# The head of a fused transformer block: six of sixteen input tiles transposed on TensorE, the LayerNorm scale split over three engines, the large head loads on one queue

## The chip, the cores and the metric

The kernel runs on one core of one Trainium2 chip. The metric is device time in microseconds (us) of one execution. Before the change it was 1218.61 us (median of its first three runs, 1215.19 to 1218.82).

The engines are named as the profile names them: PE is TensorE's matmul, PEld its weight load (the two overlap), DVE is VectorE, ACT is ScalarE, POOL is GpSimd and SP is SyncE. In this kernel SP only starts DMA transfers.

## The reference, cut to what matters

```python
x = A_x                                        # 1 x 2048 x 1024, bf16
h = x + attention(layernorm(x), wq, wk, wv, wo)   # 32 query heads of 32, ONE key/value head
h2 = h + mlp(layernorm(h), w_gate, w_up, w_down)  # sigmoid(g) * u, 3584 hidden columns

def _layernorm(x, axis=-1, eps=1e-5):
    m = jnp.mean(x, axis=axis, keepdims=True)
    v = jnp.var(x, axis=axis, keepdims=True)
    return (x - m) / jnp.sqrt(v + eps)
```

The 2048 rows are 16 tiles of 128 rows. Softmax in the attention covers all 2048 keys, so every tile of x must be normalised, transposed and multiplied by wk and wv before the first PV product can run.

## The kernel before

The program is written by a small planner. It holds a guess of each instruction's duration, walks through the work by priority, and so fixes, once and for all, the order of the instructions on each engine. On the chip each engine runs its own list in that order and waits on semaphores. A time that changes on the chip does not reorder anything, but a change in the planner's input does.

The head (the part that the change touches) loads x on two queues, computes the statistics, normalises in two passes, and transposes each tile by a DMA:

```python
load_x([0], SP, "sp"); load_x([1], SP, "sp"); load_x([2, 3], SP, "sp")
# wk, wv: on ACT's queue
load_x([4, 5, 6, 7], ACT, "act")
load_wq(0)                                 # ACT's queue
load_x([8, 9, 10, 11], ACT, "act")
load_x([12, 13, 14, 15], ACT, "act")
load_wq(1)                                 # ACT's queue
warm = pl.op("act", lambda: ACT.activation(out=tnh[:, 0, 0:1], in_=half, func=ACTF.Exp), ...)
wo_ld = dma(lambda: SP.dma_start(wo_sb[:, :, :], ...), "wo", D * D * 2, [x_ld[12]], prio=4)
...
for ts in [[0], [1]] + [[t, t + 1] for t in range(2, NT, 2)]:
    sv = stats(0, ts, ...)                 # DVE: bn_stats; POOL: two powers give rstd
    for t in ts:
        cen = ... DVE.tensor_scalar(..., scalar1=mvr[:, 0, t, 0:1], op0=ALU.subtract) ...
        if t < 1 or t >= 10:
            xnorm[t] = ... DVE.tensor_scalar(..., scalar1=rstd[:, 0, t:t + 1], op0=ALU.mult) ...
        else:
            xnorm[t] = ... ACT.activation(..., func=ACTF.Copy, scale=rstd[:, 0, t:t + 1]) ...
        xT_ev[t] = dma(lambda t=t: SP.dma_start_transpose(
            out=xnT4[t // 4][:, :, (t % 4) * P:(t % 4 + 1) * P], in_=x_sb[:, t, :]), ...)
```

After that, five kinds of TensorE work run. They are named in the order of the planner's priorities:

```python
PRIO = ["KV", "Q0", "PV", "OP", "D", "GU", "Q"]
```

KV and Q are the projections (KV gives the keys and the values). Then there are the scores and PV, the attention proper, with an exp on ScalarE between them. OP is the output projection of a tile, GU the gate and up half of the MLP, D its down half. The MLP goes in *chunks*: tile 0 and tile 1 alone, then two tiles at a time.

The softmax here doesn't subtract the row's maximum and nothing guards it: scores larger than these inputs give would overflow.

Of the kernel before, what the change touches and what calls it, by code (L numbers as in the profile page):

```python
# [35 lines left out]
class Plan:  # L36
# [39 lines left out]
    def step(self, limit):  # L76
        best = None
        for e in self.ENG:
            h = self.heap[e]
            if h:  # L80
                s = max(self.free[e], min(o.ready for o in h))
                if best is None or s < best[0]:
                    best = (s, e)
        if best is None or (limit is not None and best[0] > limit):
            return False
        s, e = best
        h = self.heap[e]
        o = min((o for o in h if o.ready <= s + 1e-9), key=lambda o: (o.prio, o.seq))
        h.remove(o)
        self.free[e] = s + o.occ  # L90
        if o.nbytes:
            go = max(s + 1300.0, self.dma_free[e])
            self.dma_free[e] = go + o.nbytes / 260.0
            o.end = self.dma_free[e] + 700.0
        else:
            o.end = s + o.lat
        o.pos = len(self.lists[e])
        self.lists[e].append(o)
        for u in o.users:
            u.ready = max(u.ready, o.end)  # L100
            u.missing -= 1
            if u.missing == 0:
                self.heap[u.eng].append(u)
        o.users = []
        return True
# [22 lines left out]
def bass_sequential_preLN__grouped_kv_mqa__glu_gated_glu__prompt_kernel(  # L128
# [34 lines left out]
    with ExitStack() as es:  # L163
# [5 lines left out]

        zone = SB("zone", [NFT * D])  # L170
# [52 lines left out]
        def dma(fn, key, nbytes, deps=(), prio=5, ring="sp"):  # L223
            return pl.op(ring, fn, deps, occ=520.0, key=key, nbytes=nbytes, prio=prio)
# [15 lines left out]
        c_v1 = pl.op("pool", lambda: POOL.memset(Vaug[:, :, DH:DH + 1], 1.0), [c1], occ=100)  # L240
# [4 lines left out]
        def load_x(ts, eng, ring):  # L245
            sl = slice(ts[0] * P, (ts[-1] + 1) * P)
            o = dma(lambda: eng.dma_start(x_sb[:, ts[0]:ts[-1] + 1, :], xf[sl, :].rearrange("(a p) n -> p a n", p=P)),
                    f"x{ts[0]}", P * D * 2 * len(ts), prio=0, ring=ring)
            for t in ts:
                x_ld[t] = o  # L250

        def load_wq(k):
            wq_ld.append(dma(lambda: ACT.dma_start(
                wq_sb[:, :, k * 512:(k + 1) * 512],
                A_wq[:, k * 512:(k + 1) * 512].rearrange("(a p) n -> p a n", p=P)), f"wq{k}", D * 512 * 2, prio=0,
                ring="act"))

        load_x([0], SP, "sp")
        load_x([1], SP, "sp")
        load_x([2, 3], SP, "sp")  # L260
# [4 lines left out]
        load_x([4, 5, 6, 7], ACT, "act")  # L265
        load_wq(0)
        load_x([8, 9, 10, 11], ACT, "act")
        load_x([12, 13, 14, 15], ACT, "act")
        load_wq(1)
        warm = pl.op("act", lambda: ACT.activation(out=tnh[:, 0, 0:1], in_=half, func=ACTF.Exp), [c0], prio=1, occ=1400)  # L270
        wo_ld = dma(lambda: SP.dma_start(wo_sb[:, :, :], A_wo.rearrange("(g p) n -> p g n", p=P)), "wo", D * D * 2,
                    [x_ld[12]], prio=4)
# [45 lines left out]
        xT_ev = {}  # L318
        for ts in [[0], [1]] + [[t, t + 1] for t in range(2, NT, 2)]:
            sv = stats(0, ts, [x_sb[:, t, :] for t in ts], [[x_ld[t]] for t in ts], 3)  # L320
            for t in ts:
                cen = pl.op("dve", lambda t=t: DVE.tensor_scalar(
                    out=x_sb[:, t, :], in0=x_sb[:, t, :], scalar1=mvr[:, 0, t, 0:1], scalar2=None, op0=ALU.subtract),
                    [sv[0]], prio=2, occ=400, lat=560)
                if t < 1 or t >= 10:
                    xnorm[t] = pl.op("dve", lambda t=t: DVE.tensor_scalar(
                        out=x_sb[:, t, :], in0=x_sb[:, t, :], scalar1=rstd[:, 0, t:t + 1], scalar2=None, op0=ALU.mult),
                        [cen, sv[1]], prio=1, occ=400, lat=560)
                else:
                    xnorm[t] = pl.op("act", lambda t=t: ACT.activation(  # L330
                        out=x_sb[:, t, :], in_=x_sb[:, t, :], func=ACTF.Copy, scale=rstd[:, 0, t:t + 1]),
                        [cen, sv[1]], prio=1, **t_act(1024))
                xT_ev[t] = dma(lambda t=t: SP.dma_start_transpose(
                    out=xnT4[t // 4][:, :, (t % 4) * P:(t % 4 + 1) * P], in_=x_sb[:, t, :]), f"xT{t}", P * D * 2, [xnorm[t]], prio=0)
# [8 lines left out]
        PRIO = ["KV", "Q0", "PV", "OP", "D", "GU", "Q"]  # L343

        def mm(o, l, r, start, stop, **kw):
            return lambda: PE.matmul(o, lhsT=l, rhs=r, start=start, stop=stop, **kw)  # L346

# [170 lines left out]
        def mk_PV(G):  # L518
# [12 lines left out]
            def after(b, last):  # L531
# [11 lines left out]
                if g == NG - 1:  # L543
                    ot_ev[qb] = dma(lambda: SP.dma_start_transpose(out=OT[:, qb % 2, :, :], in_=Osb[:, qb % 2, :]),
                                    f"OT{qb % 2}", P * D * 2, [o_ev[qb * NG + i] for i in range(NG)] + [op_last.get(qb - 2)],
                                    prio=0)
# [54 lines left out]
        def flush_hT():  # L601
            while late_hT and (CHUNK_OF[late_hT[0]] == 0 or (CHUNK_OF[late_hT[0]] - 1) in gu_last):
# [4 lines left out]
                    [hnorm[t], gu_last.get(c - 1)], prio=0)  # L607
# [86 lines left out]
        for t in range(NT):  # L694
            queue_after_xT(t)
        for t in range(2):
            load_xr(t, [])
        for s in range(NSLAB):
            load_slab(s, [xT_ev[k] for k in range(4 * s, 4 * s + 4)] if s < 4 else [xT_ev[NT - 1]])
# [168 lines left out]
```

## Time and profile before

| | before |
|---|---|
| time | 1218.61 us |
| PE busy | 1143.3 us of 1219.1 (94%) |
| ACT busy | 1041.3 us (85%) |
| PE idle in the first 80 us | 33.8 us |
| first projection matmul | 24.97 us |

These lines are from the page of the kernel before: the busy table, and the table of 40 slices, each 30.5 us wide, with the busy share in tenths.

```profile
span 1219.1 us, 47282 instructions
PE 1143.3 (94%) x21988; PEld 820.6 (67%) x22080; DVE 289.2 (24%) x788; ACT 1041.3 (85%) x1316; POOL 38.4 (3%) x82
...
PE   1889888989889999999999999999999999999998
...
ACT  2769988999999999999999999999999999991120
...
PEclk9989998999899999999999999999999999999999
DMA  8972499299136551566326651568135650579480
```

PE's first slice is the worst.

The waits of PE in the first 80 us, as total us, times, longest:

```profile
PE F_ps L346 <- DMA zone<-ring: 26.6, 3, 25.0
PE F_ps L346 <- ACT QTb L235: 4.0, 4, 1.6
PE F_ps L346 <- issue: 2.7, 1, 2.7
```

`zone<-ring` is the DMA transpose of a normalised x tile. The first projection takes tiles 0 and 1 together, so it waits for both transposes, until 25.0 us. Two lines of the chain that ended last show where these 25 us went, as start, us, what: the load of x, then the transposes.

```profile
1.84 9.02 DMA ring<-in_A_x_dram
...
14.72 10.01 DMA zone<-ring
```

Tile 1 was normalised, and its transpose issued, at 14.7 us; the result came 10 us later. The windows view gives 46.24 us of PE busy in the first 80:

```profile
sum 80.00, PE 46.24 PEld 32.76 DVE 38.09 ACT 40.88 POOL 16.85; mean PE 5.78 PEld 4.09 DVE 4.76 ACT 5.11 POOL 2.11
```

ScalarE's timeline (start, us, instruction) shows its own late start. It was held by issuing large loads until 10.9 us:

```profile
4.02 4.64 ACTq L247 DMA_DIRECT2D ring<-in_A_x_dram  x2
8.69 2.21 ACTq L253 DMA_DIRECT2D zone<-in_A_wq_dram  x1
10.93 1.28 ACT L270 ACT_TABLE_LOAD   x1 [10.93 <-issue]
```

### The profile page before, as it was taken

Reading aid. Unit: us, or ns where it says so; the run is one execution under the profiler, and the core shown is the slowest. Engines: PE = TensorE matmul, PEld = TensorE weight load, DVE = VectorE, ACT = ScalarE, POOL = GpSimd, SP = SyncE. Lnnn points to the kernel's source line nnn. Section 1 sums busy time; section 2 is a strip of 40 time slices with the busy share of each in tenths; the row PEclk is TensorE's granted clock in tenths of the full one; section 3 lists DMA queues with packets and bytes.
Section 4 is the critical chain, followed back from the end, with each engine's and each line's share of the span. In section 5 each row is a group of like instructions: output and inputs, shape, how many; then the busy total and the mean of one; then the engine's idle time right before and its main releaser. Section 6 shows DMA issues by size and latency. Waiting matters only on the chain.

```text
span 1219.1 us, 47282 instructions
## 1 busy us (share of the span) xinstructions
PE 1143.3 (94%) x21988; PEld 820.6 (67%) x22080; DVE 289.2 (24%) x788; ACT 1041.3 (85%) x1316; POOL 38.4 (3%) x82
## 2 busy tenths in 40 slices
PE   1889888989889999999999999999999999999998
PEld 1645576676568765877577865787567865787684
DVE  8222211222121312121212112221212221222121
ACT  2769988999999999999999999999999999991120
POOL 4100000000000000000000000000000000000000
PEclk9989998999899999999999999999999999999999
DMA  8972499299136551566326651568135650579480
GB/s 263 227 209 95 130 271 266 67 252 250 48 89 180 152 136 41 153 176 168 73 80 158 175 144 33 149 183 186 52 80 158 179 141 15 115 193 219 112 213 18
DMA packets 338308, 178.29 MB, mean 146 GB/s; under 512 B 58304, under 2 KB 328640, under 8 KB 338112
## 3 DMA queue, kind: packets, MB, share of 16 engines
q1 hardware_dynamic: 332368, 169.90, 54.1%
q10 hardware_dynamic: 5744, 5.37, 1.3%
q8 instruction: 173, 2.83, 1.0%
q14 instruction: 23, 0.19, 0.0%
HBM read 155.32 MB, written 7.34 MB: 133 GB/s over the span
## 4 chain that ended last, share of the span: by engine, by line
PE 85%; ACT 7%; issue 3%; DMA 3%; DVE 1%; ACTq 0%; DVEq 0%
PE F_ps L346 72%; PE S_ps L346 13%; ACT Pr L503 6%; DMA zone<-ring 2%; DMA ring<-in_A_x_dram 1%; DMA q_scratch<-hact 1%; ACT tnh L647 1%; ACT ring L330 1%; DVE hact L654 0%; DMA hnT<-hn 0%; DVE st L285 0%; DVE st L287 0%; DVE h_sb L580 0%; ACT QTb L235 0%; DVE mv L289 0%
## 5 line engine op out<-in xcount | busy, mean ns | idle before, releaser
L503 ACT ACTIVATE Pr<-S_ps 128x1024 bf16<-128x1024 f32 x1024 | 977.9, 1042 | 39.6 <-PE S_ps L346 38.7
L346 PE MATMUL F_ps<-hnT,ring 128*128 128x256 bf16 (+1 forms) x4032 | 445.9, 262 | 4.7 <-issue 1.6
L346 PEld LDWEIGHTS F_ps<-hnT,ring 128*128 128x128 bf16 x4032 | 340.6, 98 | 61.3 <-issue 5.9
L346 PE MATMUL F_ps<-Vaug,Pr 128*128 128x33 bf16 x8192 | 244.9, 178 | 9.8 <-issue 7.3
L346 PEld LDWEIGHTS F_ps<-Vaug,Pr 128*128 128x128 bf16 x8192 | 229.6, 96 | 35.9 <-issue 8.9
L346 PE MATMUL S_ps<-QTb,kT 32*128 32x128 bf16 x8192 | 208.8, 218 | 18.5 <-ACT Pr L503 10.9
L346 PEld LDWEIGHTS S_ps<-QTb,kT 32*128 32x128 bf16 x8192 | 119.7, 93 | 130.7 <-ACT Pr L503 73.5
L346 PE MATMUL F_ps<-zone,hact 128*128 128x512 bf16 x843 | 203.2, 380 | 3.8 <-issue 1.8
L654 DVE SCALAR_TENSOR_TENSOR hact<-tnh,F_ps 128x256 bf16<-128x256 f32 (+1 forms) x252 | 97.7, 391 | 445.0 <-ACT tnh L647 436.6
L647 ACT ACTIVATE tnh<-F_ps 128x256 f32<-128x256 f32 (+1 forms) x252 | 94.5, 380 | 81.3 <-PE F_ps L346 81.3
L346 PEld LDWEIGHTS F_ps<-zone,hact 128*128 128x128 bf16 x896 | 78.9, 98 | 88.5 <-DVE hact L654 0.3
L346 PE MATMUL F_ps<-zone 128*128 128x256 bf16 (+2 forms) x497 | 73.2, 294 | 31.9 <-DMA zone<-ring 26.6
L346 PEld LDWEIGHTS F_ps<-zone 128*128 128x128 bf16 x512 | 38.5, 99 | 53.3 <-issue 27.5
L686 DVE SCALAR_TENSOR_TENSOR h_sb<-F_ps,h_sb 128x512 bf16<-128x512 f32 x32 | 22.1, 692 | 199.4 <-PE F_ps L346 199.4
L346 PE MATMUL F_ps<-wo_sb,OT 128*128 128x512 bf16 x232 | 60.7, 390 | 4.1 <-issue 2.1
L536 DVE RECIPROCAL rL<-F_ps 128x4 f32<-128x4 f32 x128 | 23.4, 183 | 149.2 <-PE F_ps L346 149.1
L299 POOL TENSOR_SCALAR zb<-mvb 128x1 bf16<-128x1 bf16 (+1 forms) x25 | 5.6, 224 | 1073.3 <-DVE mvb L295 1073.3
L346 PEld LDWEIGHTS F_ps<-wo_sb,OT 128*128 128x128 bf16 x256 | 22.0, 99 | 25.4 <-issue 4.9
L538 DVE TENSOR_TENSOR Osb<-F_ps,rL 128x128 bf16<-128x128 f32 x128 | 37.3, 291 | 4.3
L580 DVE TENSOR_TENSOR h_sb<-F_ps,xres 128x512 bf16<-128x512 f32 x32 | 22.1, 692 | 56.3 <-PE F_ps L346 56.3
L236 DVE CAST hact<-F_ps 128x512 bf16<-128x512 f32 x24 | 16.6, 692 | 39.4 <-PE F_ps L346 37.3
L306 POOL TENSOR_TENSOR rstd<-dsb,cst 128x1 f32<-128x1 bf16 (+1 forms) x25 | 16.7, 667 | 1.9
(27 smaller groups left out, 116.7 us busy)
## 6 DMA issues: line engine op xcount, KB each, us to landing
ring<-in_B_w_gate_dram SPq DMA_DIRECT2D x126, 512.0 KB, 4.2
ring<-in_B_w_up_dram SPq DMA_DIRECT2D x126, 512.0 KB, 5.8
zone<-in_B_w_down_dram SPq DMA_DIRECT2D x7, 1024.0 KB, 7.6
xres<-in_A_x_dram SPq DMA_DIRECT2D x16, 256.0 KB, 2.7
out_dram<-h_sb SPq DMA_DIRECT2D x32, 128.0 KB, 1.7
ring<-in_A_x_dram ACTq DMA_DIRECT2D x3, 1024.0 KB, 12.6
q_scratch<-hact SPq DMA_DIRECT2D x24, 128.0 KB, 2.4
QTb<-q_scratch SPq DMA_DIRECT2D x6, 512.0 KB, 3.5
```

Of the source, the lines that this page charges most:

```text
L236: lambda: DVE.tensor_copy(out=out_ap, in_=in_ap))
L299: f = pl.op("pool", lambda: POOL.tensor_scalar(out=zb[:, ph, sl].unsqueeze(2), in0=mvb[:, ph, sl, 1:2], scalar1=LN_EPS_BF16, scalar2=None, ...
L306: h = pl.op("pool", lambda: POOL.tensor_tensor(out=rstd[:, ph, sl], in0=dsb[:, ph, sl], in1=nb, op=ALU.pow), [g, c1], prio=prio - 1, occ=5 ...
L330: xnorm[t] = pl.op("act", lambda t=t: ACT.activation(out=x_sb[:, t, :], in_=x_sb[:, t, :], func=ACTF.Copy, scale=rstd[:, 0, t:t + 1]), [ce ...
L346: return lambda: PE.matmul(o, lhsT=l, rhs=r, start=start, stop=stop, **kw)
L503: exps[u] = pl.op("act", lambda slot=slot, pb=pb: ACT.activation(out=Pr[:, slot, :].rearrange("p (a b) -> p a b", a=2), in_=S_ps[:, pb:pb ...
L536: a = pl.op("dve", lambda: DVE.reciprocal(rL[:, k, :].unsqueeze(2), ov[:, :, DH:DH + 1]), [last], prio=0, occ=70, lat=280)
L538: e = pl.op("dve", lambda: DVE.tensor_tensor(out=Osb[:, qb % 2, g * P:(g + 1) * P].rearrange("p (a b) -> p a b", a=4), in0=ov[:, :, 0:DH], ...
L580: h_ev[(t, dc)] = pl.op("dve", lambda: DVE.tensor_tensor(out=h_sb[:, t % 4, sl], in0=F_ps[:, b, :], in1=xres[:, t % 2, sl], op=ALU.add), [ ...
L647: a = pl.op("act", lambda: ACT.activation(out=tnh[:, k, 0:n], in_=F_ps[:, b, 0:n], func=ACTF.Tanh, scale=0.5), [last, tn_user.get(k)], pri ...
L654: e = pl.op("dve", lambda: DVE.scalar_tensor_tensor(out=hactT[:, ft, 0:n], in0=tnh[:, k, 0:n], scalar=1.0, in1=F_ps[:, b, 256:256 + n], op ...
L686: e = pl.op("dve", lambda: DVE.scalar_tensor_tensor(out=h_sb[:, t % 4, sl], in0=F_ps[:, b, :], scalar=0.5, in1=h_sb[:, t % 4, sl], op0=ALU ...
```

## The change

The intent is to let TensorE begin earlier: tiles 0 to 5 are transposed on TensorE, so they do not queue among DMA loads; ScalarE issues only the two small loads; ScalarE and VectorE give some of the scaling to GpSimd; and the weights that are needed later are loaded behind the transposes. The planner's guesses of DMA time are adjusted too (bandwidth 260 to 280, a DMA transpose's issue 520 to 1330 ns), and so is that of a VectorE pass over a tile (400 to 360 ns).

```diff
-            self.dma_free[e] = go + o.nbytes / 260.0
+            self.dma_free[e] = go + o.nbytes / 280.0
...
-        load_x([4, 5, 6, 7], ACT, "act")
+        load_x([2, 3])                    # all load_x and load_wq on SP now
+        load_x([4, 5])
+        load_x([6, 7])
         load_wq(0)
...
-        wo_ld = dma(..., [x_ld[12]], prio=4)
...
+        SCALE_ON = ["dve"] + ["act"] * 3 + ["pool"] * 2 + ["act"] + ["pool"] * 2 + ["act"] + ["pool"] * 2 + ["dve"] * 4
...
+        wo_ld = dma(..., [xnorm[NT - 1]], prio=4)
...
-        PRIO = ["KV", "Q0", "PV", "OP", "D", "GU", "Q"]
+        PRIO = ["xT", "KV", "Q0", "PV", "OP", "D", "GU", "Q"]
...
+        def mk_xT(t):                     # eight 128x128 transposes into one PSUM bank
+            ...
+                return [(lambda dt=dt: PE.transpose(out=tp[:, dt * P:(dt + 1) * P],
+                                                    in_=x_sb[:, t, dt * P:(dt + 1) * P], identity=ident[:, :]),
+                         P, []) for dt in range(DT)]
+            ...
+                xT_ev[t] = pl.op("act", fa, [last], prio=2, **t_act(1024))    # evicted by ScalarE
+                if t == NPT - 1:          # then the ten DMA transposes, then the MLP weight slabs
+                    for k in range(NPT, NT):
+                        dma_xT(k)
+                    for k in range(4):
+                        load_slab(k, ...)
...
+        NPT = 6
```

More of the change, by code (lines that the diff above doesn't have):

```diff
@@ L168, in SB @@
             return EC(nc.sbuf_tensor(name, [P] + shape, dt))
+        ident = SB("ident", [P])
         zone = SB("zone", [NFT * D])
@@ L221, in bass_sequential_preLN__grouped_kv_mqa__glu_gated_glu__prompt_kernel, with dma @@
         PE, ACT, DVE, POOL, SP = nc.tensor, nc.scalar, nc.vector, nc.gpsimd, nc.sync
-        def dma(fn, key, nbytes, deps=(), prio=5, ring="sp"):
-            return pl.op(ring, fn, deps, occ=520.0, key=key, nbytes=nbytes, prio=prio)
+        def dma(fn, key, nbytes, deps=(), prio=5, ring="sp", occ=520.0):
+            return pl.op(ring, fn, deps, occ=occ, key=key, nbytes=nbytes, prio=prio)
         def evac(fn_act, fn_dve, n, deps, prio, dve_rate=0.96):
@@ L239, in bass_sequential_preLN__grouped_kv_mqa__glu_gated_glu__prompt_kernel, with load_x @@
         c1 = pl.op("pool", lambda: POOL.memset(negone, -1.0), [c0], occ=60)
-        c_v1 = pl.op("pool", lambda: POOL.memset(Vaug[:, :, DH:DH + 1], 1.0), [c1], occ=100)
+        c2 = pl.op("pool", lambda: POOL.memset(ident[:, :], 0.0), [c1], occ=200)
+        c_id = pl.op("pool", lambda: POOL.affine_select(
+            out=ident[:, :], in_=ident[:, :], compare_op=ALU.not_equal, fill=1.0, base=0,
+            pattern=[[-1, P]], channel_multiplier=1), [c2], occ=300)
+        c_v1 = pl.op("pool", lambda: POOL.memset(Vaug[:, :, DH:DH + 1], 1.0), [c_id], occ=100)
         x_ld = {}
         wq_ld = []
-        def load_x(ts, eng, ring):
+        def load_x(ts):
             sl = slice(ts[0] * P, (ts[-1] + 1) * P)
-            o = dma(lambda: eng.dma_start(x_sb[:, ts[0]:ts[-1] + 1, :], xf[sl, :].rearrange("(a p) n -> p a n", p=P)),
-                    f"x{ts[0]}", P * D * 2 * len(ts), prio=0, ring=ring)
+            o = dma(lambda: SP.dma_start(x_sb[:, ts[0]:ts[-1] + 1, :], xf[sl, :].rearrange("(a p) n -> p a n", p=P)),
+                    f"x{ts[0]}", P * D * 2 * len(ts), prio=0)
             for t in ts:
@@ L252, in load_wq @@
         def load_wq(k):
-            wq_ld.append(dma(lambda: ACT.dma_start(
+            wq_ld.append(dma(lambda: SP.dma_start(
                 wq_sb[:, :, k * 512:(k + 1) * 512],
-                A_wq[:, k * 512:(k + 1) * 512].rearrange("(a p) n -> p a n", p=P)), f"wq{k}", D * 512 * 2, prio=0,
-                ring="act"))
-        load_x([0], SP, "sp")
-        load_x([1], SP, "sp")
-        load_x([2, 3], SP, "sp")
+                A_wq[:, k * 512:(k + 1) * 512].rearrange("(a p) n -> p a n", p=P)), f"wq{k}", D * 512 * 2, prio=0))
+        load_x([0])
+        load_x([1])
         wk_ld = dma(lambda: ACT.dma_start(wk_sb, A_wk.rearrange("(a p) j -> p a j", p=P)), "wk", P * DT * DH * 6, prio=0,
@@ L264, in bass_sequential_preLN__grouped_kv_mqa__glu_gated_glu__prompt_kernel @@
                     ring="act")
-        load_x([4, 5, 6, 7], ACT, "act")
+        load_x([2, 3])
+        load_x([4, 5])
+        load_x([6, 7])
         load_wq(0)
-        load_x([8, 9, 10, 11], ACT, "act")
-        load_x([12, 13, 14, 15], ACT, "act")
+        load_x([8, 9])
+        load_x([10, 11])
+        load_x([12, 13, 14, 15])
         load_wq(1)
         warm = pl.op("act", lambda: ACT.activation(out=tnh[:, 0, 0:1], in_=half, func=ACTF.Exp), [c0], prio=1, occ=1400)
-        wo_ld = dma(lambda: SP.dma_start(wo_sb[:, :, :], A_wo.rearrange("(g p) n -> p g n", p=P)), "wo", D * D * 2,
-                    [x_ld[12]], prio=4)
         rep = None
@@ L321, in bass_sequential_preLN__grouped_kv_mqa__glu_gated_glu__prompt_kernel @@
             for t in ts:
-                cen = pl.op("dve", lambda t=t: DVE.tensor_scalar(
-                    out=x_sb[:, t, :], in0=x_sb[:, t, :], scalar1=mvr[:, 0, t, 0:1], scalar2=None, op0=ALU.subtract),
-                    [sv[0]], prio=2, occ=400, lat=560)
-                if t < 1 or t >= 10:
-                    xnorm[t] = pl.op("dve", lambda t=t: DVE.tensor_scalar(
-                        out=x_sb[:, t, :], in0=x_sb[:, t, :], scalar1=rstd[:, 0, t:t + 1], scalar2=None, op0=ALU.mult),
-                        [cen, sv[1]], prio=1, occ=400, lat=560)
-                else:
-                    xnorm[t] = pl.op("act", lambda t=t: ACT.activation(
-                        out=x_sb[:, t, :], in_=x_sb[:, t, :], func=ACTF.Copy, scale=rstd[:, 0, t:t + 1]),
-                        [cen, sv[1]], prio=1, **t_act(1024))
-                xT_ev[t] = dma(lambda t=t: SP.dma_start_transpose(
-                    out=xnT4[t // 4][:, :, (t % 4) * P:(t % 4 + 1) * P], in_=x_sb[:, t, :]), f"xT{t}", P * D * 2, [xnorm[t]], prio=0)
+                xt, sc = x_sb[:, t, :], rstd[:, 0, t:t + 1]
+                cen = pl.op("dve", lambda t=t, xt=xt: DVE.tensor_scalar(
+                    out=xt, in0=xt, scalar1=mvr[:, 0, t, 0:1], scalar2=None, op0=ALU.subtract),
+                    [sv[0]], prio=2, occ=360, lat=560)
+                if SCALE_ON[t] == "act":
+                    xnorm[t] = pl.op("act", lambda xt=xt, sc=sc: ACT.activation(out=xt, in_=xt, func=ACTF.Copy, scale=sc),
+                                     [cen, sv[1]], prio=1, **t_act(1024))
+                else:
+                    eng, cost = (DVE, dict(occ=360, lat=560)) if SCALE_ON[t] == "dve" else (POOL, dict(occ=1500, lat=1650))
+                    xnorm[t] = pl.op(SCALE_ON[t], lambda xt=xt, sc=sc, eng=eng: eng.tensor_scalar(
+                        out=xt, in0=xt, scalar1=sc, scalar2=None, op0=ALU.mult), [cen, sv[1]], prio=1, **cost)
+        wo_ld = dma(lambda: SP.dma_start(wo_sb[:, :, :], A_wo.rearrange("(g p) n -> p g n", p=P)), "wo", D * D * 2,
+                    [xnorm[NT - 1]], prio=4)
         bank_rel = [[], []]
@@ L342, in bass_sequential_preLN__grouped_kv_mqa__glu_gated_glu__prompt_kernel, with atoms, after, dma_xT @@
         queues = collections.defaultdict(collections.deque)
-        PRIO = ["KV", "Q0", "PV", "OP", "D", "GU", "Q"]
+        PRIO = ["xT", "KV", "Q0", "PV", "OP", "D", "GU", "Q"]
         def mm(o, l, r, start, stop, **kw):
             return lambda: PE.matmul(o, lhsT=l, rhs=r, start=start, stop=stop, **kw)
+        def mk_xT(t):
+            def atoms(b):
+                tp = F_ps[:, b, :].bitcast(BF16)
+                return [(lambda dt=dt: PE.transpose(out=tp[:, dt * P:(dt + 1) * P],
+                                                    in_=x_sb[:, t, dt * P:(dt + 1) * P], identity=ident[:, :]),
+                         P, []) for dt in range(DT)]
+            def after(b, last):
+                src = F_ps[:, b, :].bitcast(BF16).rearrange("p (a b) -> p a b", a=DT)
+                fa, fd = both(xnT4[t // 4][:, :, (t % 4) * P:(t % 4 + 1) * P], src)
+                xT_ev[t] = pl.op("act", fa, [last], prio=2, **t_act(1024))
+                xT_pe[t] = last
+                queue_after_xT(t)
+                if t == NPT - 1:
+                    for k in range(NPT, NT):
+                        dma_xT(k)
+                    for k in range(4):
+                        load_slab(k, [xT_pe[j] for j in range(4 * k, 4 * k + 4)] + [xT_ev[NT - 1]])
+                    for k in range(4, NSLAB):
+                        load_slab(k, [xT_ev[NT - 1]])
+                return [xT_ev[t]]
+            return Group("xT", atoms, lambda: [xnorm[t], c_id], after)
+        xT_pe = {}
+        NPT = 6
+        def dma_xT(t):
+            xT_ev[t] = dma(lambda: SP.dma_start_transpose(
+                out=xnT4[t // 4][:, :, (t % 4) * P:(t % 4 + 1) * P], in_=x_sb[:, t, :]), f"xT{t}", P * D * 2,
+                [xnorm[t]], prio=0, occ=1330.0)
+            xT_pe[t] = xT_ev[t]
+            queue_after_xT(t)
         def queue_after_xT(t):
@@ L545, in after @@
                                     f"OT{qb % 2}", P * D * 2, [o_ev[qb * NG + i] for i in range(NG)] + [op_last.get(qb - 2)],
-                                    prio=0)
+                                    prio=0, occ=1330.0)
                     for dc in range(2):
@@ L606, in flush_hT @@
                     out=hnT[:, :, i * P:(i + 1) * P], in_=hn[:, t % 2, :]), f"hT{t % 2}", P * D * 2,
-                    [hnorm[t], gu_last.get(c - 1)], prio=0)
+                    [hnorm[t], gu_last.get(c - 1)], prio=0, occ=1330.0)
                 if t == CH[c][-1]:
@@ L694, in bass_sequential_preLN__grouped_kv_mqa__glu_gated_glu__prompt_kernel @@
         for t in range(NT):
-            queue_after_xT(t)
+            if t < NPT:
+                queues["xT"].append(mk_xT(t))
         for t in range(2):
-            load_xr(t, [])
-        for s in range(NSLAB):
-            load_slab(s, [xT_ev[k] for k in range(4 * s, 4 * s + 4)] if s < 4 else [xT_ev[NT - 1]])
+            load_xr(t, [xnorm[NT - 1]])
         cur = None
```

## The prediction

> **What bounds it now.** TensorE: busy 1143.3 of 1219.1 us (94%, busy table), ScalarE 1041.3 (85%); the final chain is 85% PE. From 80 us on both are nearly full (10-us windows). The loss is in the head. In the windows of the first 80 us PE is busy about 46 us, so idle 34: its first matmul comes at 24.97 us (timeline; waits view: 25.0 us for the crossbar transposes of x), about 9 us follow in gaps. First exp 35.5 us. The last key/value group waits for a transpose until 61.5; the first PV matmul, which needs all of V, runs at 67. The chain view: x load until 10.9, VectorE stats, then DMA transposes for 10.0, later 4.2 and 5.0 us. They queue on SyncE among wo (11.5 us to landing) and weight slabs.
>
> **What the change does.**
> - ScalarE is freed of five large loads, whose issue held it until its table load at 10.93 us. The Trainium skill (DMA: Bandwidth & Descriptors, "Issuing engines are not separate DMA queues") says that several issuing engines save issue time only; so no bandwidth change, only ScalarE ready near 5 us.
> - Tiles 0 to 5 go through 48 PE transposes (estimate 0.1 us each, from 98 ns weight loads: 5 us, mostly in idle PE time) and six ScalarE evictions (about 1.04 us, as the 128x1024 exp), in place of crossbar transposes landing in 3.2 to 11.1 us.
> - ScalarE scales 5 tiles instead of 9 (1.14 us each): 10.3 us become 5.7 + 6.2, even.
> - GpSimd scales six tiles. The Trainium skill (GPSIMD Engine Reference, "Engine selection") calls one-input work roughly line-rate there; estimate 1 to 1.5 us each, between its power steps (0.7 and 1.0 us); may delay the next rstd by 1 to 3 us.
> - VectorE keeps its 37 us of head work (bn_stats 21.4, subtract 7.0); it was full from 3.6 to 37 us, so tile 15 is still ready only at 36 to 39 us.
> - wo, residual and slab loads are issued behind all transposes. DMA has room later (share 0.3 between 80 and 140 us).
>
> **On the critical path (estimates).** First PE transpose at 9.5, first key/value matmul near 15 us (was 25), first exp near 23 (35.5), last key/value group near 43 (61.5), first PV near 47 (67). PE does not gain 20 us: projections it did while waiting have still to be done. PE idle: 34 before; after, about 15 before the first useful matmul, 3 for later transposes, 8 to 10 of waits for ScalarE evictions behind scales and exps. So 6 to 8 us, up to 15 if the gaps are smaller; some more from earlier exps. Work after the head is unchanged, with its own stalls (8.7 us for the q stores behind w_down near 150 us), and moves up.
>
> **Predicted: 1208 us, 1198 to 1218 (8 in 10). Faster by over 2%: 0.06; within 2%: 0.92; slower: 0.02.**
>
> **Right if** PE's first key/value matmul is at 13 to 17 us, no PE wait for a transpose of tiles 6 to 15 exceeds 3 us, PE idle in the first 80 us is 20 to 28 us, and the rest only shifts. **Wrong if** GpSimd's scales take over 2 us or slow VectorE's subtract through shared ports (then tile 15 is past 42 us); if ScalarE becomes the head's bottleneck; if the later weight loads collide with the first GU chunk; or if reordered stalls between 140 and 300 us outweigh the head's gain.

## More of the kernel before

The attention goes tile by tile. A tile is 8 *head groups* (four heads each), a head group needs 4 score steps, 8 exps of 128x1024 and 64 PV matmuls.

```python
CH = [[0], [1]] + [[t, t + 1] for t in range(2, NT, 2)]
...
# GU of chunk c: needs hnT of all its tiles, that is OP, the second LayerNorm and a DMA transpose
gr = Group("GU", atoms, lambda: [hT_ev[t] for t in CH[c]] + slab_ld[s], after)
```

So the chunk of tiles 2 and 3, the first full one, needs 4 x 8 = 32 head groups of attention to be done.

## The result

After the change the kernel takes 1202.04 us (median of four runs, 1201.13 to 1203.51), against 1218.28 us before (four runs, 1215.19 to 1218.82). The ratio is 0.9873, with a 95% interval of 0.9853 to 0.9893. Ratios in this document are the mean time of one kernel's runs over that of the other's of the same rounds, so they are not quite the ratio of the medians quoted. By the bounds of 2% the class is "same", but the gain of about 16 us is real: the two ranges are 12 us apart.

The page of the kernel after:

```profile
span 1200.6 us, 47381 instructions
PE 1145.9 (95%) x22038; PEld 823.6 (69%) x22128; DVE 295.0 (25%) x794; ACT 1040.1 (87%) x1310; POOL 55.0 (5%) x90
...
PE   4789989999899999999999999999999999999998
...
ACT  5689999999999999999999999999999999991120
...
PEclk9999989999899999999999999999999999999999
DMA  6883299589256623755156732667146640569480
```

PE has as much work as before, and ends sooner. The first slice went from 1 to 4 tenths, as it should. But look further right: before, slices 5, 7, 9 and 12 (335 to 366 us) were at 8, now they are at 9, and slice 11 is the last at 8. The change touched no code that runs there.

PE's waits in the first 80 us:

```profile
PE F_ps L357 <- POOL rstd L310: 10.1, 1, 10.1
PE F_ps L352 <- DMA zone<-ring: 4.5, 3, 2.5
PE F_ps L352 <- issue: 4.1, 3, 3.8
PE F_ps L352 <- ACT QTb L236: 2.9, 1, 2.9
```

The 26.6 us of waits for DMA transposes are 4.5 now. PE's timeline has the transposes (line 357) and the first projection at 15.40 (it was 24.97):

```profile
10.07 1.03 PE L357 MATMUL F_ps<-ident,ring 128*128 128x128 bf16 x8 [10.07 <-POOL rstd L310]
...
15.40 2.32 PE L352 MATMUL F_ps<-zone 128*128 128x256 bf16 x24 [1.12 <-ACT zone L236]
```

ScalarE loads its table at 1.84 us instead of 10.93:

```profile
1.84 1.28 ACT L276 ACT_TABLE_LOAD   x1 [1.84 <-issue]
```

And the first 80 us hold 53.88 us of PE work, so idle time went from 33.8 to 26.1 us:

```profile
sum 80.00, PE 53.88 PEld 39.66 DVE 43.04 ACT 49.84 POOL 33.43; mean PE 6.74 PEld 4.96 DVE 5.38 ACT 6.23 POOL 4.18
```

That is 7.6 us less idle time in the head, and the 48 new transposes keep PE busy for 5.7 us. The head can't explain 16 us in this plain way. To see where the time came from, compare when the same piece of work is done. The times are from the two traces; the end of an exp or an eviction marks the step.

| done at (us) | before | after | difference |
|---|---|---|---|
| last keys evicted (the last values follow 0.3 us later) | 63.4 | 54.1 | -9.3 |
| exp 64 (attention of tile 0) | 119.6 | 109.4 | -10.3 |
| last Q projection | 142.9 | 148.0 | +5.1 |
| first GU of tile 0 | 146.8 | 152.4 | +5.6 |
| exp 256 (attention of tile 3) | 322.3 | 300.4 | -21.9 |
| D of tile 1 (MLP of tiles 0 and 1 done) | 318.0 | 312.3 | -5.7 |
| first GU of tiles 2 and 3 | 350.8 | 331.1 | -19.7 |
| last GU | 1192.4 | 1173.9 | -18.5 |

Two streams of work move at different rates. The attention is 10 us ahead at its 64th exp and 22 us ahead at its 256th. The MLP is *late* at first, and ahead by 5.7 us when tiles 0 and 1 are done. Then, in the stretch between "D of tile 1" and "first GU of tiles 2 and 3", the difference jumps from 5.7 to 19.7 us. That stretch was 32.8 us before and is 18.8 after. From there to the end both kernels take the same time: 868.3 and 869.5 us to the end of the span.

So look at that stretch, the *hand-over* from the MLP of tile 1 to that of tiles 2 and 3. The windows view, for the kernel before and then for the kernel after:

```profile
318.00:351.00 33.00, 22.45 (x570) 15.55 (x571) 5.78 (x18) 30.17 (x34) 1.34 (x3) 0.84 0.19 47
```

```profile
312.00:331.00 19.00, 16.04 (x356) 10.91 (x354) 5.37 (x15) 17.89 (x21) 1.36 (x3) 0.82 0.16 37
```

The columns after the length are busy us of PE, PEld, DVE, ACT and POOL, then the granted clock. Before, PE is idle for 10.6 of 33 us while ACT is nearly full (30.17). PE's waits there, before and then after:

```profile
PE S_ps L346 <- ACT Pr L503: 6.3, 7, 1.5
```

```profile
PE S_ps L352 <- ACT Pr L542: 2.4, 2, 1.4
```

The chain that ended last, of the kernel before, says the same. From 307.4 us on it runs over ScalarE's exps, not over PE:

```profile
307.40 7.44 ACT Pr L503 x8
...
314.86 7.45 ACT Pr L503 x8
```

PE had done the MLP of tiles 0 and 1. The MLP of tiles 2 and 3 could not start, because the attention of tile 3 was not finished. The attention alone goes at ScalarE's pace, about 1.04 us an exp. After the change the attention of tile 3 was done by then: its output projection (`wo_sb`) starts behind D at once, at 313.7 us, where before it started at 329.1. PE's timeline, before and then after:

```profile
329.13 1.06 PE L346 MATMUL F_ps<-wo_sb,OT 128*128 128x512 bf16 x2 [1.57 <-issue]
```

```profile
313.68 0.59 PE L352 MATMUL F_ps<-wo_sb,OT 128*128 128x512 bf16 x2
```

This can be counted exactly, since the order is fixed. A head group has 64 PV weight loads. Up to the last matmul of D of tile 1, at 316.8 us before and 311.1 us after, the groups view of PEld counts:

```profile
L346 PEld LDWEIGHTS F_ps<-Vaug,Pr 128*128 128x128 bf16 x1920 | 53.5, 96 | 16.8 <-issue 8.2 <-DVE hact L654 2.7
```

```profile
L352 PEld LDWEIGHTS F_ps<-Vaug,Pr 128*128 128x128 bf16 x2048 | 56.9, 96 | 12.8 <-issue 4.4 <-DVE hact L693 1.5
```

1920 / 64 = 30 head groups before, 2048 / 64 = 32 after; 32 are needed. **The program before was two head groups short at this hand-over, and the program after is not.** Two groups are 16 exps, at 1042 ns each 16.7 us of ScalarE: an estimate, from the mean in the groups view, of what the missing groups cost where nothing else can fill PE. The stretch shrank by 14.0 us.

This reading was found in the traces. The experiments are needed to tell whether it, or something else in the change, carries the gain.

### The profile page after: what moved, and what is told of

Read it like the earlier page. It is cut to its first block, busy times and chain, and to the rows that moved or that the text cites. A ratio compares the mean times of both kernels' runs of the same rounds, so it can differ in the third digit from the quotient of the medians. Undisturbed runs are those within 1.5% of the kernel's fastest.

```text
span 1200.6 us, 47381 instructions
## 1 busy us (share of the span) xinstructions
PE 1145.9 (95%) x22038; PEld 823.6 (69%) x22128; DVE 295.0 (25%) x794; ACT 1040.1 (87%) x1310; POOL 55.0 (5%) x90
## 4 chain that ended last, share of the span: by engine, by line
PE 81%; ACT 10%; issue 3%; POOL 2%; DMA 2%; DVE 1%; SPq 0%; ACTq 0%; POOLq 0%; DVEq 0%
PE F_ps L352 69%; PE S_ps L352 12%; ACT Pr L542 10%; POOL ring L336 1%; ACT tnh L686 1%; DMA q_scratch<-hact 1%; DMA zone<-ring 1%; DMA ring<-in_A_x_dram 0%; DVE st L289 0%; DVE st L291 0%; POOL rstd L310 0%; POOL dsb L308 0%; DVE hact L693 0%; DVE ring L328 0%; DVE h_sb L619 0%
## 5 line engine op out<-in xcount | busy, mean ns | idle before, releaser
L237 DVE CAST hact<-F_ps 128x512 bf16<-128x512 f32 x24 | 16.6, 692 | 37.4 <-PE F_ps L352 35.3
L357 PE MATMUL F_ps<-ident,ring 128*128 128x128 bf16 x48 | 5.7, 294 | 13.3 <-POOL rstd L310 10.1
```

Source lines behind the costliest of these rows:

```text
L237: lambda: DVE.tensor_copy(out=out_ap, in_=in_ap))
L357: return [(lambda dt=dt: PE.transpose(out=tp[:, dt * P:(dt + 1) * P], in_=x_sb[:, t, dt * P:(dt + 1) * P], identity=ident[:, :]), P, []) f ...
```

## The experiments

All twelve kernels gave correct results, each timed in three rounds. The theories, as the expectations use or describe them:

- **H** (head): the rebuilt head earns the gain; in the prediction's form, fewer idle us of TensorE in the head are the gain, one for one.
- **P**: the planner's new constants reorder the rest, and the head has little to do with it.
- **F**: TensorE's stops for instruction fetch (shown below) fall at other places by chance. Its rival **D** in the expectations says that these stops are waits for data.
- **L**: the attention's lead over the MLP decides, at the hand-over to tiles 2 and 3. Its rival **W** holds that work on TensorE alone counts, so that a delay on ScalarE would be hidden.

The "dry stretch from D 4 to GU 57" of the expectations is the stretch above: from the end of D of tile 1 (the fourth D group) to the first GU result of tiles 2 and 3 (the 57th).

### Planner constants alone

`b_const` is the kernel before with the new constants; `a_oldconst` is the kernel after with the old ones.

```diff
-            self.dma_free[e] = go + o.nbytes / 260.0
+            self.dma_free[e] = go + o.nbytes / 280.0
...                                # and occ 520 -> 1330 for the DMA transposes
```

> The kernel before with only the planner's constants of the change (DMA rate 280 for 260; 1330 for 520 ns of SyncE per crossbar transpose). Theory H (the head rebuild earns the gain, about 10 us of it by exp 64, the rest by a reshuffled middle): within 4 us of before, 1214 to 1222 us, exp 64 done at 118 to 121 us as before. Rival P (the planner's better constants reorder the middle and earn the 11 us between exp 96 and exp 192): 1205 to 1210 us, exp 96 to exp 192 in 95 to 98 us where before took 107.

> The kernel after with the planner's old constants (260 and 520). Theory H: 1200 to 1208 us, exp 64 still near 109 us. Rival P: the middle falls back to 107 us from exp 96 to exp 192, and the time to 1211 to 1215 us.

`b_const`: 1213.87 us (just under the range of H) against 1218.01, ratio 0.9966 (0.9942 to 0.9989). `a_oldconst`: 1202.22 us, ratio 0.9875 (0.9843 to 0.9907), as the full change. The constants are worth about 4 us on the kernel before and nothing on the kernel after. P falls.

### No transposes on TensorE

`a_dma16` keeps everything else of the change, but all sixteen tiles go by DMA, as before. (The edit also loads the slabs behind the transposes, as the kernel after does; those lines are left out here.)

```diff
-            if t < NPT:
-                queues["xT"].append(mk_xT(t))
+            dma_xT(t)
```

> The kernel after with no TensorE transposes: all sixteen tiles by crossbar DMA, everything else as after. If the TensorE transposes are what starts the head early: first key/value matmul back from 15 to about 20 us, exp 64 at 113 to 117 us, time 1206 to 1211 us. If the order of SyncE's queue (wo, residual and weight slabs behind all transposes) is what counts: first key/value matmul near 17 us, exp 64 within 2 us of 109.4, time 1199 to 1205 us.

1219.40 us (1212.41 to 1221.37), ratio 0.9995 (0.9951 to 1.0039): both expectations are missed, the whole gain is gone. PE's waits in its first 80 us:

```profile
PE F_ps L352 <- DMA zone<-ring: 23.9, 1, 23.9
```

The first DMA transpose was issued at 9.97 us. Issuing it held SyncE for 8.2 us, and it landed at 21.96 us, just behind the last head load (21.1 us). The second, which the first projection needs too, landed at 23.67. Of the 6.3 MB of x and wq, an estimated 3.7 MB were still to come at 9.97 us (from the windows view: 2.6 MB moved until then). PE is idle for 35.3 of the first 80 us. Yet its 64th exp ended at 110.1 us, as early as in the kernel after (109.4). It got there by putting projections off: the last one ended at 160.0 us (148.0), and D of tile 1 at 333.6 us (312.3). The attention had done 33 head groups by then, so the stretch was 18.8 us, but the MLP came 21 us late. An early exp, bought by putting other work off, was worth nothing.

### GpSimd's scales given to VectorE

`a_nopool` moves the six scales, and nothing else. `a_nopool_pe8` also transposes eight tiles on TensorE.

```diff
-        SCALE_ON = ["dve"] + ["act"] * 3 + ["pool"] * 2 + ["act"] + ["pool"] * 2 + ["act"] + ["pool"] * 2 + ["dve"] * 4
+        SCALE_ON = ["dve"] + ["act"] * 3 + ["dve"] * 2 + ["act"] + ["dve"] * 2 + ["act"] + ["dve"] * 6
```

> The kernel after with GpSimd's six scales (2.90 us each in its trace) given to VectorE (0.48 us each). If GpSimd's scales held VectorE and the power steps back: VectorE's copies of the mean return from 0.53 to 0.16 us and its subtract from 0.58 to 0.48 us, tile 15 is ready at 37 to 41 us instead of 45.5, the last key/value group at 44 to 48 us instead of 54, time 1195 to 1201 us. If they were off the critical path: 1200 to 1205 us.

> A try for a better version: GpSimd's scales on VectorE and eight tiles on TensorE instead of six. Head idle 18 to 21 us (a_nopool: 21.9); time 1196 to 1202 us if the middle keeps it, 1201 to 1206 us if the instruction fetches and the DMA-bound weight stream take it again.

The groups view of the first 60 us: GpSimd's scale, VectorE's subtract and VectorE's cast of the means back to f32, in the kernel after (count, then total us and mean ns):

```profile
L336 POOL TENSOR_SCALAR ring<-ring,rstd 128x1024 bf16<-128x1024 bf16 x6 | 17.3, 2896 | 0.7 <-POOL rstd L310 0.7
...
L328 DVE TENSOR_SCALAR ring<-ring,mvr 128x1024 bf16<-128x1024 bf16 x16 | 8.6, 576 | 0.0
...
L301 DVE CAST mvr<-mvb 128x4 f32<-128x4 bf16 x7 | 3.7, 532 | 0.0
```

The same VectorE lines in `a_nopool`, with the scale that took GpSimd's place:

```profile
L328 DVE TENSOR_SCALAR ring<-ring,mvr 128x1024 bf16<-128x1024 bf16 x16 | 7.0, 475 | 0.0
L336 DVE TENSOR_SCALAR ring<-ring,rstd 128x1024 bf16<-128x1024 bf16 x11 | 4.9, 480 | 0.6
...
L301 DVE CAST mvr<-mvb 128x4 f32<-128x4 bf16 x7 | 1.1, 152 | 0.0
```

A scale took 2896 ns on GpSimd (two that follow each other start 2.84 us apart) and takes 480 ns on VectorE. With GpSimd's scales in the kernel, the mean of VectorE's subtract is 576 ns instead of 475, and that of the small cast 532 instead of 152. These means hide two kinds of instruction. The four casts that overlap a GpSimd scale took 0.68 to 1.00 us, the others 0.11 to 0.15. Of the six subtracts that overlap one, two took 1.25 and 1.32 us, and four took 0.46 to 0.49, as without GpSimd. VectorE's timeline of the kernel after has a cast between two GpSimd scales, and one that falls into the scale from 30.29 to 33.30 us:

```profile
23.53 0.15 DVE L301 CAST mvr<-mvb 128x4 f32<-128x4 bf16 x1
...
30.42 1.00 DVE L301 CAST mvr<-mvb 128x4 f32<-128x4 bf16 x1
```

So the prediction's doubt about GpSimd was right: over 2 us each, and VectorE slowed. Without it tile 15 is ready at 42.3 us (45.5 in the kernel after; 37 to 41 expected), all keys are evicted at 49.6 us (54.1), exp 64 ends at 105.0 (109.4), and PE is idle for 21.9 us of the first 80 (26.1).

And the time did not move: 1203.00 us (1200.38 to 1204.71), ratio 0.9875 (0.9846 to 0.9903). `a_nopool_pe8`, with only 19.8 us of idle head, took 1204.49 us, ratio 0.9871 (0.9852 to 0.9891). The view of the head alone falls here: 4 to 6 us less idle time on TensorE in the head gave nothing. Both have 32 head groups done at the hand-over, exactly as the kernel after.

### The same programs again

`a_shift` and `b_shift` were meant to move the positions of TensorE's instructions by 128 do-nothing instructions, to test F.

```diff
         def _(eng):
+            for _i in range(128):
+                eng.nop()
             emit("pe", eng)
```

> The kernel after with 128 do-nothing instructions put in front of TensorE's stream (TensorE is idle there until 10 us); nothing else changes, so its 16-KB instruction fetches fall at other places. Theory F (the stalls in the middle of matmul groups between 140 us and GU 57 are instruction fetches on full DMA rings, a matter of where they fall): the stalls move to other groups, each still ending 1.3 to 1.7 us after a fetch packet, and the time moves by up to 5 us either way, 1199 to 1208 us. Rival D (the stalls are waits for weight slabs or other data): the same stalls at the same groups and 1200 to 1204 us.

> The kernel before with the same 128 do-nothing instructions. Theory F: the 13.8 us of such stalls of before are partly luck; they move and their sum changes by some us, time 1210 to 1221 us. If the middle is luck through and through, before could come within 6 us of after. Rival D: same stalls, 1215 to 1221 us.

The test failed in its construction. The do-nothing instructions never reached the program: the instruction counts of the pages are unchanged (47381 and 47282), and the packets of the "instruction" queue (below) start at the same places in TensorE's list (median difference 0 instructions). F's own test is thus missing. So these are repeats: 1201.15 us (1199.72 to 1204.01; ratio 0.9864) and 1216.58 us (1214.59 to 1218.11; ratio 0.9987, 0.9958 to 1.0016). They give the noise of the middle: in the profiled runs, the first GU of tiles 2 and 3 came at 350.8 and 346.3 us for one and the same kernel before, and at 331.1 and 335.2 for the kernel after.

The noise has a visible form. TensorE stops inside a group of matmuls, waiting for nothing that the profile names, as in this timeline of the kernel before:

```profile
251.42 0.39 PE L346 MATMUL S_ps<-QTb,kT 32*128 32x128 bf16 x13 [0.16 <-ACT Pr L503]
254.21 0.23 PE L346 MATMUL S_ps<-QTb,kT 32*128 32x128 bf16 x3 [2.40 <-issue]
```

This stop ended 1.5 us after a 16 KB packet of the queue marked "instruction" had landed (251.56 to 252.71), in a moment when the DMA engines were full. The kernel before has five such stops of over 1 us before 350 us where the packet's end is 1.3 to 1.6 us before the restart, 10.8 us in sum; the kernel after has three (1.4 to 1.7 us), 6.2 us in sum. In the two traces of one kernel not all of them come again: the sums of the repeats are 5.4 us (`b_shift`) and 7.0 us (`a_shift`). That PE waits there for its own instructions is argued from these times, not shown by an experiment. As the cause of the gain F does not stand: `b_shift` has the least of these stops among the four traces, and its profiled run is still 13.0 us longer than that of `a_shift` (1215.2 and 1202.2 us).

### The last w_down loads put behind the q stores

The prediction named a stall near 150 us in which the first GU results wait for stores queued behind weight loads. `a_qfix` orders them the other way; `a_nopool_qfix` has both edits.

```diff
-                free_wd(last)
+                if q_left[0] > 0:
+                    free_wd(last)
...
                 if q_left[0] == 0:
+                    free_wd(ev)
                     load_q(2)
```

> The kernel after with the last four w_down loads issued behind the last q store instead of ahead of it. If the store's wait in the rings costs what it seems (VectorE's first hact waits 7 us, TensorE idles about 4 us around 153 to 158 us, then 6.8 us at half clock): 1194 to 1199 us, and no half-clock stretch near 156 us. If the rings are full anyway: 1200 to 1204 us.

> Both: GpSimd's scales on VectorE and the w_down loads behind the last q store. If the head's 4 us of a_nopool were only lost again in the middle: 1192 to 1198 us. If the middle absorbs whatever the head gains: as a_qfix within 2 us.

The stall did vanish: from 145 to 162 us PE was busy for 16.50 us (12.67 in the kernel after), and the eighth GU was done at 165.4 us instead of 172.1. The kernel got slower: 1211.63 us (1209.52 to 1213.93), ratio 0.9948 (0.9915 to 0.9980). `a_nopool_qfix`: 1205.62 us (1203.87 to 1208.10), ratio 0.9905 (0.987 to 0.994). Both miss. Only in `a_qfix` is the attention one group short at the hand-over. Up to the last matmul of D of tile 1:

```profile
L352 PEld LDWEIGHTS F_ps<-Vaug,Pr 128*128 128x128 bf16 x1984 | 55.4, 96 | 17.0 <-issue 9.3 <-DVE hact L695 1.6
```

1984 / 64 = 31. Its stretch is 25.2 us instead of 18.8, and the rest of its loss lies ahead of it (D of tile 1 at 320.6 us). Why that D came 8 us late was not traced.

### The attention held back on purpose

`a_lag` is the kernel after with nine exps whose results nobody reads, put on ScalarE behind exp 34: 9.3 us of delay for the attention, none for TensorE's head.

```diff
+            if v == 16:
+                jk = exps[2 * v + 1]
+                for _ in range(9):
+                    jk = pl.op("act", lambda: ACT.activation(out=junk[:, :], in_=kT4[:, 0:1024], func=ACTF.Exp, scale=SCALE),
+                               [jk], prio=0, **t_act(1024))
```

> The kernel after with nine idle exps (9.3 us of ScalarE work into a buffer that nobody reads) put once into ScalarE's list after exp 34, known to the planner. It takes the attention's lead away and leaves TensorE's head and work alone. Theory L (the head's gain is paid out twice: 7.6 us of TensorE idle in the head, and again at 310 to 350 us, because attention that is 10 us ahead shortens the stretch in which the MLP has run dry and waits for tiles 2 and 3): exp 96 about 9 us later than in after, the dry stretch from D 4 to GU 57 grows from 18.8 to 27 to 34 us and its idle from 3 to 8 to 11 us, time 1207 to 1213 us. Rival W (total TensorE work alone sets the time, and ScalarE has slack to catch up): 1200 to 1205 us, dry stretch under 22 us.

1221.66 us (1218.96 to 1222.27), ratio 1.0010 (0.9991 to 1.0029): the whole gain is gone, 20 us for 9.3 us of delay on an engine that has 160 us of idle time in the span. W falls. The idle time in the head stays at 24.9 us. The MLP is even *earlier* than in any other kernel (D of tile 1 at 307.8 us). But only 29 groups are done at that point:

```profile
L353 PEld LDWEIGHTS F_ps<-Vaug,Pr 128*128 128x128 bf16 x1857 | 51.3, 96 | 11.4 <-issue 4.2 <-DVE hact L699 1.3 <-DVE hact L238 0.7
```

(The one over 29 x 64 = 1856 is the first of the next group.) And the stretch is the worst of all, 41.5 us, with PE at a mean clock of 0.67:

```profile
308.00:350.00 42.00, 28.92 (x716) 19.84 (x707) 6.46 (x19) 38.00 (x42) 1.34 (x3) 0.67 0.14 37
```

The direction is as L expected, the size is larger than expected. The planner knew of the idle exps, so they did two things at once: they delayed ScalarE, and they made the planner place the MLP earlier in TensorE's order. Which share each has was not separated.

### The head loads, and the transposes alone

`a_actloads` is the kernel after with the large head loads back on ScalarE's and SyncE's queues. `b_pe6` is the kernel before with the six transposes on TensorE and the slab loads behind them, and nothing else of the change: old queues, old split of the scales, old constants, wo and residual early. (Only the planner's guess of a VectorE pass, 360 ns for 400, stayed as in the kernel after.)

```diff
-        load_x([4, 5])
-        load_x([6, 7])
+        load_x([4, 5, 6, 7], ACT, "act")
...                                # load_x 8 to 15 and load_wq likewise
```

> The kernel after with the head's loads issued by ScalarE and SyncE in the old order and sizes, as before. If freeing ScalarE's queue counts: its first eviction comes later than 11.1 us by 1 us or more and the time is 1204 to 1208 us. If it does not (ScalarE has its first tile to evict only at 11.1 us, and the old issue ended at 10.9): within 3 us of after, 1199 to 1205 us.

> The kernel before plus the six TensorE transposes (and the slab loads behind them), all else as before: loads on ScalarE, old split of the scale, wo and residual early, old planner constants. If the TensorE transposes are the change: 1199 to 1206 us, dry stretch 18 to 22 us. If they need the rest: 1208 to 1214 us.

`a_actloads`: 1200.65 us (1198.91 to 1203.20), ratio 0.9844 (0.9822 to 0.9865). Moving the loads is worth nothing here, though it let ScalarE's table load come 7.7 us earlier (1.84 us in the kernel after, 9.56 here). This agrees with the Trainium skill (DMA: Bandwidth & Descriptors, "Issuing engines are not separate DMA queues"), which says that more issuing engines save only the time of issuing.

`b_pe6`: 1196.99 us (1192.63 to 1206.38), ratio 0.9831 (0.9777 to 0.9884). The transposes on TensorE, with the slab loads behind them, carry the whole gain; `a_dma16`, with the slab loads behind its transposes but none on TensorE, has nothing of it. Its median is the lowest of all, but the spread is wide: the mean of its four runs is 1198.2 us, that of `a_actloads` beside it 1200.9. That it beats the kernel after is not shown. Its head is much better than that of the kernel after, because the slow GpSimd scales are not in it:

```profile
sum 80.00, PE 58.05 PEld 42.78 DVE 44.40 ACT 62.46 POOL 17.36; mean PE 7.26 PEld 5.35 DVE 5.55 ACT 7.81 POOL 2.17
```

PE is idle for 22.0 us there, exp 64 ends at 98.5 us, and 33 head groups are done at the hand-over. Still the stretch is 18.8 us, as in the kernel after.

### All of them in one table

"Groups" is the number of head groups in TensorE's order ahead of the last matmul of D of tile 1; "D" is the end of that step and "gap" the time from there to the first GU result of tiles 2 and 3; "rest" is from there to the end of the span. All are from the profiled run of each kernel, in us.

| kernel | median | idle in first 80 | D of tile 1 | groups | gap | rest |
|---|---|---|---|---|---|---|
| before | 1218.28 | 33.8 | 318.0 | 30 | 32.8 | 868.3 |
| b_shift (repeat of before) | 1216.58 | 33.5 | 313.5 | 30 | 32.8 | 868.9 |
| b_const | 1213.87 | 34.9 | 311.9 | 30 | 33.1 | 867.3 |
| a_lag | 1221.66 | 24.9 | 307.8 | 29 | 41.5 | 871.2 |
| a_qfix | 1211.63 | 26.8 | 320.6 | 31 | 25.2 | 866.3 |
| after | 1202.04 | 26.1 | 312.3 | 32 | 18.8 | 869.5 |
| a_shift (repeat of after) | 1201.15 | 26.0 | 316.4 | 32 | 18.8 | 867.0 |
| a_oldconst | 1202.22 | 23.5 | 312.1 | 32 | 17.9 | 868.5 |
| a_actloads | 1200.65 | 26.7 | 314.3 | 32 | 18.7 | 867.1 |
| a_nopool | 1203.00 | 21.9 | 315.9 | 32 | 18.8 | 868.0 |
| a_nopool_pe8 | 1204.49 | 19.8 | 316.0 | 32 | 19.8 | 867.5 |
| a_nopool_qfix | 1205.62 | 23.3 | 315.9 | 32 | 18.8 | 867.3 |
| b_pe6 | 1196.99 | 22.0 | 310.2 | 33 | 18.8 | 864.4 |
| a_dma16 | 1219.40 | 35.3 | 333.6 | 33 | 18.8 | 866.1 |

Read the columns from right to left. The rest is the same everywhere, within 7 us. The gap is a function of the count of groups: 41.5, 32.8 to 33.1, 25.2, then 17.9 to 19.8 us for 29, 30, 31 and 32 or more. Each missing group costs 6.4 to 8.7 us; an estimate from 8 exps of 1.042 us is 8.3. From 32 on, more lead brings nothing. And D of tile 1, in spite of 7 us less idle head, hardly moved: its mean is 314.5 us in the three traces of the old head with 30 groups and 313.8 in the four of the new head as it stands (after, a_shift, a_oldconst, a_actloads). What idle time TensorE lost went into transposes and into two more head groups, which are done by then. The sums agree: up to that D, PE is idle for 50.4 us on average in the three old traces (34.1 of them in the first 80 us) and for 38.4 (25.6) in the four new ones. The difference of 12.0 us is about what 48 transposes (5.7 us) and two head groups (3.5 us each, by the estimate below) take.

## Why the prediction was right or wrong

The time (1208 predicted, 1202.04 measured) lies in the range, and the class was right. That is in part luck: the gain was 16 us and not 10, and most of it came at a place for which the prediction's sum has no number. The reasons, point by point:

- **"From 80 us on both are nearly full", only in part.** It holds from 80 to 140 us (PE busy for 58.8 of 60). But from 80 us to D of tile 1 PE was idle for 20.8 us, and for 10.6 in the stretch behind it, together nearly as much as in the head (33.8). So the hand-over was not looked at.
- **The first matmul, right.** First PE transpose at 10.07 us (9.5 predicted), first projection at 15.40 (near 15). The longest wait for a DMA transpose was 2.5 us (at most 3). PE idle in the first 80 us was 26.1 us (20 to 28).
- **Issue engines, right in saying that bandwidth does not change; the benefit of an early ScalarE is nil.** From 10 to 20 us the DMA engines moved 370 GB/s before and 369 after. ScalarE was ready at 5.35 us (near 5), and `a_actloads` shows this to be worth nothing.
- **GpSimd, mis-sized.** The estimate of 1 to 1.5 us rested on the skill's page (GPSIMD Engine Reference, "Engine selection": one-input work is roughly line-rate); the trace has 2.90 us. The prediction had scales of over 2 us, or a slowed subtract on VectorE, among what would make it wrong, and both came true (the subtract in two of sixteen tiles): tile 15 was ready at 45.5 us, not at 36 to 39, and the last keys were evicted at 54.1, not near 43; first exp 27.3 instead of near 23, first PV 57.1 instead of 47. It did not cost the kernel time, since the head had lead to spare (`a_nopool`). So a condition that was named as fatal came true and was harmless.
- **"PE idle ... So 6 to 8 us, up to 15": the idle time was right (7.6 us), its price was not.** The failed step is "Work after the head is unchanged ... and moves up", which takes each idle us of TensorE as one us of time. The runs show two prices. Ahead of the hand-over nothing moved (D of tile 1 314.5 and 313.8 us on average). At the hand-over two head groups no longer had to be waited for, which gave 14.0 us (32.8 to 18.8), nearly all of the gain. A head group is about 3.5 us of TensorE (208.8 + 244.9 us of scores and PV over 128 groups), but 6.4 to 8.7 us if it is missing where only ScalarE can make progress. The term "some more from earlier exps" was the place for this; it was left without a number.
- **That stalls between 140 and 300 us could outweigh the gain** did not happen, but they are what blurs it: two traces of one kernel differ by 4 to 5 us there.

Open: what the order alone would do with unchanged times (in `a_lag` order and delay change together), and whether the stops of TensorE are its instruction fetch. The gap's dependence on the groups rests on fourteen traces, in one of which (`a_lag`) the lead was set on purpose; 29 and 31 groups were seen once each.

The count of groups needed no chip. Both programs could be built, and the order of TensorE's list read, before the prediction; it has 30 and 32 groups ahead of that D.

## What to carry to other kernels

Where two streams feed one engine and the second has a hand-over to the first (here the MLP of a tile pair that needs its attention), find the hand-over and count, in the fixed order of the program, how much of the slower stream is done by then; here a missing unit cost 6.4 to 8.7 us, near its pace on the slow engine, and lead beyond the needed count was worth nothing. Transposes that are needed first did badly here in DMA queues full of loads (first projection at 24.97 and, in `a_dma16`, 23.9 us); on TensorE they began at 10.07 us and the projection at 15.40. And undo a combined change one part at a time: here one part of five (`b_pe6`) carried everything, one (GpSimd's scales) delayed the keys by 4.5 us without a change of the time, and the removal of a plainly visible stall (`a_qfix`) made the kernel slower.

## What the Trainium skill lacked or had wrong

- GPSIMD Engine Reference, section 4.1, "Engine selection", calls one-input elementwise work roughly line-rate on GpSimd. A bf16 scale of 128x1024 by a per-row scalar took 2896 ns there, 480 ns on VectorE and about 1140 ns on ScalarE.
- The same page, section 1, "Specifications", says that GpSimd shares its memory interface with VectorE in some modes, without a size there (other pages of the skill treat this further). Here the mean of a VectorE subtract of 128x1024 went from 475 to 576 ns and that of a cast of 128x4 from 152 to 532 ns: four casts that overlapped a GpSimd scale took 0.68 to 1.00 us, and two subtracts 1.25 and 1.32 us, while four other overlapping subtracts took no longer than alone.
- TensorE: Matmul & The Clock Gate, Part 4, gives about 275 ns for a transpose in a kernel, 390 ns alone, and no rate for a row of them. The profile's mean of one is 294 ns, but eight back to back took 1.03 us for the first tile and 0.62 us for the sixth.
- VectorE: DVE Perf Modes, "The three transpose paths", gives one figure (1309 ns, for 128x128) for a DMA transpose. One of 128x1024 landed 3.0 to 4.8 us after its issue in the kernel after, where the head loads were through, but 12.0 us after it in `a_dma16`, where an estimated 3.7 MB of them were still to come. That section doesn't say what loads ahead in the queue cost.
- Runtime: NRT & Kernel Launch, "Instruction fetch mechanics", says that an engine's instructions are refilled in blocks of 16 KiB, but has no length for a stop in which a block comes late. Stops of TensorE that ended 1.3 to 1.7 us after a 16 KB packet of the "instruction" DMA queue took 1.2 to 3.8 us here and summed to 10.8 us before and 6.2 us after, and not all came again in a repeat of the same program. That they are such late blocks is not shown.
